# Splitting the transposing loads of two input matrices into rows 0-511 and 512-639

## The chip, the cores and the metric

One core of a Trainium2 chip. The time is the device time of the kernel in microseconds (us), as the median of several executions. The profile and the trace are of one execution: its span, from the first to the last instruction, is some 1.3 us shorter than the time that is measured for the same execution. PE is the matrix engine (TensorE), PEld its weight loads, DVE VectorE, ACT ScalarE, POOL GpSimd, SP the engine that issues most transfers.

## The reference, cut to what matters

The kernel computes a gated mix of a state space model (a) and a dense layer with GELU (b), for 2048 tokens of width 640:

```python
g = sigmoid((x * gate_w).sum(-1, keepdims=True))
Bu   = einsum("bld,pd->blp", x, B_bar)     # complex: B_re, B_im, both 640 x 640
h[t] = Lam_bar * h[t-1] + Bu[t]            # a scan along the tokens
a = 2.0 * einsum("blp,dp->bld", h, C).real + x * Dskip
b = gelu(x @ w1 + b1) @ w2 + b2
out = g * a + (1 - g) * b
```

The change concerns how B_re and B_im come into the core. As stored, a row is an output p and a column an input d; PE needs d on the partitions, so both are transposed while they are loaded.

## The kernel before

The kernel plans all its operations, sorts them by priority per engine and then emits them. Tokens of data (such as `("BT", 0)`) tie an operation to the load that it needs. The four parts that the argument touches, shortened:

```python
def load_T(name, sem, pairs, writes, prio, dur, lat=3.0, reads=()):
    def fn():
        for dst, src in pairs:
            t = dma_inc("sp", nc.sync.dma_start_transpose(dst, src), sem)
        return t
    return op(name, "sp", dur, reads, writes, fn, prio=prio, lat=lat)

def f_warm():                                   # keeps PE busy from 0.8 us on
    for n in (512,) * 6 + (256,):
        t = nc.tensor.matmul(PS[4][:, 0:n], one..., one..., start=True, stop=True)

for ci, src in enumerate((A_B_re, A_B_im)):     # the loads that are changed
    load_T(f"B{ci}", f"l_B{ci}", [(BT[:, ci, :, :], src)], [("BT", ci)], prio=30 + ci, dur=4.1)
xtrans(1, range(KD), 32, 3.4)                   # next block of x, transposed too
... (cut: gate weights, xnb, w2, C and so on, all on the same queue)

def bproj(q):                                   # 10 groups of 5 matmuls
    for ci in range(2):
        for k in range(KP):                     # KP = 5 blocks of 128 rows of B
            ... (cut: five matmuls over kd with BT[:, ci, kd, k*128:(k+1)*128] and xT[q])
            op(f"b_{q}_{k}{ci}", "pe", KD * d_mm(512), XT[q] + [("BT", ci)], [("bank", bank)], f_mm, ...)
```

PE's order at the start is: warm-up, eight 128-column transposes (L427), the first dense layer "m1" on the first block of tokens (L639 and L661, with the small L446 between), then the ten groups of `bproj(0)` (L704).

Of the kernel before, what the change touches and what calls it, by code (L numbers as in the profile page):

```python
# [147 lines left out]
class Prog:  # L148
# [8 lines left out]
    def op(self, name, eng, dur, reads, writes, fn, prio=None, lat=0.0, after=()):  # L157
        deps = {}
        for k in reads:
            for w in self.last_w.get(k, ()):  # L160
                deps[w.idx] = w
        for k in writes:
            for w in self.last_w.get(k, ()):
                deps[w.idx] = w
            for r in self.last_r.get(k, ()):
                deps[r.idx] = r
        for a in after:
            deps[a.idx] = a
        deps = list(deps.values())
        E = self.E  # L170

        def run(eg, deps=deps, eng=eng, fn=fn):
            E.wait(eng, *[d.done for d in deps if not (eng == "pe" and d.eng == "pe")])
            return fn()

        it = self.sch.add(name, eng, dur, deps, run, prio=prio, lat=lat)
        for k in writes:
            self.last_w[k] = [it]
            self.last_r[k] = []
        for k in reads:  # L180
            self.last_r.setdefault(k, []).append(it)
        return it


def bass_gated_mix__ssm_conv_s5__dense_activation_gelu__prompt_kernel(
# [18 lines left out]
    _, S, D = A_x.shape  # L204
# [3 lines left out]
    KD = D // 128  # L208
    KP = P // 128
# [16 lines left out]
    with ExitStack() as es:  # L226

        def SB(name, shape, dt):
            return es.enter_context(nc.sbuf_tensor(name, list(shape), dt))
# [5 lines left out]
        BT = SB("BT", [128, 2, KD, P], BF16)  # L235
# [72 lines left out]
        op = pr.op  # L308

        def inc(eng, ins):  # L310
            return E.inc(eng, ins, eng + "_s")

        def dma_inc(eng, ins, sem):
            SEM(sem)
            E.count.setdefault(sem, 0)
            ins.then_inc(sems[sem], 16)
            E.count[sem] += 16
            return (sem, E.count[sem])

        def d_act(n):  # L320
            return 0.26 + n * 0.00084
# [4 lines left out]
        def d_mm(n):  # L326
            return n / 2400.0 + 0.004
# [8 lines left out]
        def load_T(name, sem, pairs, writes, prio, dur, lat=3.0, reads=()):  # L336
            def fn():
                t = None
# [4 lines that stand above are left out]
# [10 lines left out]
        def xtrans(q, ks, prio, dur):  # L353
            load_T(f"xT{q}_{ks[0]}", f"l_xT{q}_{ks[0]}", [(xT[q][:, ks[0]:ks[-1] + 1, :], x2[q * 512:(q + 1) * 512, ks[0] * 128:(ks[-1] + 1) * 128])],
                   [("xT", q, k) for k in ks], prio, dur)
# [33 lines left out]
        for i, (nm, (r0, src)) in enumerate(ROWS.items()):  # L389
            src = src.rearrange("(k p) -> k p", p=128)  # L390
# [29 lines left out]
        for i, (k, c0, c1) in enumerate(((0, 0, 2), (0, 2, 4), (1, 0, 2), (1, 2, 4))):  # L420
            bank = (7, 6, 5, 4)[i]
# [18 lines left out]
        XT = {q: [("xT", q, k) for k in range(KD)] for q in range(1, NQ)}  # L440
# [137 lines left out]


        for ci, src in enumerate((A_B_re, A_B_im)):  # L580
            load_T(f"B{ci}", f"l_B{ci}", [(BT[:, ci, :, :], src)], [("BT", ci)], prio=30 + ci, dur=4.1)
        xtrans(1, range(KD), 32, 3.4)
        load("gwb", "sp", "l_gwb", gwb[:, :], gate_w.partition_broadcast(128), ["gwb"], prio=32.2)
        load("xnb", "sp", "l_xnb", xn[0][:, :, KN * 128:D], x2[0:512, KN * 128:D].rearrange("(c p) d -> p c d", p=128),
# [16 lines left out]
        def pe_prio():  # L601
            ctr["pe"] += 1
            return ctr["pe"]


        def next_bank():
            ctr["bank"] += 1
            return (ctr["bank"] - 1) % 8
# [87 lines left out]
        def bproj(q):  # L696
            for ci in range(2):
                for k in range(KP):
                    bank = next_bank()

                    def f_mm(k=k, ci=ci, bank=bank):
                        t = None
                        for kd in range(KD):
                            t = nc.tensor.matmul(PS[bank][:, :], BT[:, ci, kd, k * 128:(k + 1) * 128], xT[q][:, kd, :],  # L704
                                                 start=(kd == 0), stop=(kd == KD - 1))
                        return inc("pe", t)

                    op(f"b_{q}_{k}{ci}", "pe", KD * d_mm(512), XT[q] + [("BT", ci)], [("bank", bank)], f_mm, prio=pe_prio())

                    def f_ev(k=k, ci=ci, bank=bank):  # L710
                        dst = U[q % 2][:, :, ci, k, :]
                        src = PS[bank][:, :].rearrange("p (s t) -> p s t", s=2)
                        return inc("act", nc.scalar.activation(dst, src, ACT.Copy, scale=1.0 if ci == 0 else -1.0))  # L713

                    op(f"u_{q}_{k}{ci}", "act", d_act(512), [("bank", bank)], [("U", q % 2, k, ci)], f_ev, prio=10)
# [292 lines left out]
        m1_first()  # L1008
        m1(0, NW)
        bproj(0)  # L1010
        ssm(0)
        gates(0)
        m1(1)
        for q in range(0, NQ, 2):
            m1_tail(q)
        ssm(1)
        bproj(1)
        ssm(2)
        gates(1)
        outsT(0)  # L1020
        for q in range(2, NQ):
            ssm(2 * q - 1)
            bproj(q)
            ssm(2 * q)
            m1(q)
            xnload(q, "pool")
            gates(q)
            if q < NQ - 1:
                outsT(q - 1)
# [63 lines left out]
```

## Time and profile before

| | before |
|---|---|
| median of the first three runs | 213.13 us (212.79 to 213.13) |
| span of the profiled execution | 212.16 us |
| PE busy | 208.3 us, 98% |
| DVE busy | 190.1 us, 90% |
| real matrix: issued, landed | 9.91, 19.74 us |
| imaginary matrix: issued, landed | 16.21, 22.81 us |
| first matmul that needs them (L704) | 19.79 us |

"Landed" is when the transfer's completion semaphore has made all its 16 steps. The reading is the prediction's: a chain of work that is PE alone after 19.74, and one wait of PE for BT ahead of it. What the prediction does not show, and what will matter, is PE's timeline ahead of that wait (start, length, instructions, and in brackets the idle time before them with what ended it):

```profile
0.78 2.93 PE L415 MATMUL ps<-const-bfloat16-1.0 128*128 128x512 bf16 x7 [0.78 <-PEq L1078]
3.64 0.75 PE L427 MATMUL ps<-ident,xn 128*128 128x128 bf16 x8
5.25 2.54 PE L639 MATMUL ps<-xT,W1sb 128*128 128x256 bf16 x13 [0.86 <-DMA W1sb<-in_B_w_dram]
7.62 0.22 PE L446 MATMUL ps<-ident,rows 128*128 128x128 bf16 x1
7.68 6.42 PE L639 MATMUL ps<-xT,W1sb 128*128 128x512 bf16 x29
13.94 5.56 PE L661 MATMUL ps<-xT,W1sb 128*128 128x512 bf16 x25
```

From 5.25 us, when the first weights have come, m1 runs without a pause to 19.50. When m1 ends is therefore fixed by when it starts and by the clock in its first microseconds. Keep the 2.54 us of the first 13 matmuls of m1 in mind.

### The profile page before, as it was taken

Reading aid. Unit: us, or ns where it says so; the run is one execution under the profiler, and the core shown is the slowest. Engines: PE = TensorE matmul, PEld = TensorE weight load, DVE = VectorE, ACT = ScalarE, POOL = GpSimd, SP = SyncE. Lnnn points to the kernel's source line nnn. Section 1 sums busy time; section 2 is a strip of 40 time slices with the busy share of each in tenths; the row PEclk is TensorE's granted clock in tenths of the full one; section 3 lists DMA queues with packets and bytes.
Section 4 is the critical chain, followed back from the end, with each engine's and each line's share of the span. In section 5 each row is a group of like instructions: output and inputs, shape, how many; then the busy total and the mean of one; then the engine's idle time right before and its main releaser. Section 6 shows DMA issues by size and latency. Waiting matters only on the chain.

```text
span 212.2 us, 2747 instructions
## 1 busy us (share of the span) xinstructions
PE 208.3 (98%) x1102; PEld 104.4 (49%) x1102; DVE 190.1 (90%) x240; ACT 103.3 (49%) x177; POOL 4.2 (2%) x12
## 2 busy tenths in 40 slices
PE   6999999999999999999999999999999999999996
PEld 2444444444464444444464444444446444567775
DVE  2499999999999998999999999899999999499744
ACT  2388556679860253556681063455660027623330
POOL 1000000030000000000000000000010000000000
DMA  6899999998500020074263000009541000005251
GB/s 166 207 233 206 192 208 241 345 182 200 133 0 3 0 49 0 0 99 95 56 61 112 3 0 0 0 2 163 83 109 69 0 3 0 0 0 102 68 142 63
DMA packets 48744, 19.08 MB, mean 90 GB/s; under 512 B 41436, under 2 KB 47708, under 8 KB 48732
## 3 DMA queue, kind: packets, MB, share of 16 engines
q1 hardware_dynamic: 47072, 17.59, 39.3%
q0 software_dynamic: 1600, 1.32, 4.3%
q8 instruction: 8, 0.13, 0.3%
q14 instruction: 4, 0.03, 0.1%
q10 hardware_dynamic: 60, 0.01, 0.1%
HBM read 8.41 MB, written 2.63 MB: 52 GB/s over the span
## 4 chain that ended last, share of the span: by engine, by line
PE 90%; DMA 5%; SPq 4%; issue 0%; DVE 0%
PE ps L704 20%; PE ps L928 20%; PE ps L661 20%; PE ps L977 15%; PE ps L791 7%; PE ps L840 5%; DMA BT<-in_A_B_re_dram 5%; SPq L333 2%; SPq L340 2%; PE ps L682 1%; PE ps L939 1%; PE ps L805 0%; DVE W1sb L874 0%
## 5 line engine op out<-in xcount | busy, mean ns | idle before, releaser
L661 PE MATMUL ps<-xT,W1sb 128*128 128x512 bf16 x220 | 48.1, 379 | 0.0
L744 DVE TENSOR_TENSOR_SCAN W<-atab,V 128x1280 bf16<-128x1280 f32 x16 | 44.3, 2811 | 0.3
L704 PE MATMUL ps<-xT,BT 128*128 128x512 bf16 x200 | 43.8, 379 | 0.3 <-DMA BT<-in_A_B_re_dram 0.3
L928 PE MATMUL ps<-Gl,W2sb 128*128 128x512 bf16 (+1 forms) x234 | 42.7, 344 | 0.0
L668 ACT ACTIVATE Gl<-ps,cols 128x512 bf16<-128x512 f32 x44 | 29.9, 694 | 15.5 <-PE ps L661 15.5
L661 PEld LDWEIGHTS ps<-xT,W1sb 128*128 128x128 bf16 x220 | 21.5, 98 | 26.0
L977 PE MATMUL ps<-Hb,CT 128*128 128x512 bf16 x150 | 32.9, 379 | 0.0
L928 PEld LDWEIGHTS ps<-Gl,W2sb 128*128 128x128 bf16 x234 | 22.9, 98 | 19.3
L713 ACT ACTIVATE U<-ps 128x512 bf16<-128x512 f32 x40 | 23.7, 596 | 16.1 <-PE ps L704 16.0
L704 PEld LDWEIGHTS ps<-xT,BT 128*128 128x128 bf16 x200 | 19.4, 98 | 24.3 <-DMA BT<-in_A_B_re_dram 0.8
L946 ACT ACTIVATE E1T<-ps,cols 128x512 bf16<-128x512 f32 (+1 forms) x18 | 9.5, 624 | 36.0 <-PE ps L939 36.0
L977 PEld LDWEIGHTS ps<-Hb,CT 128*128 128x128 bf16 x150 | 14.4, 98 | 18.0 <-DVE V L496 0.6
L985 ACT ACTIVATE E2T<-ps 128x512 bf16<-128x512 f32 x15 | 9.1, 604 | 13.6 <-PE ps L977 13.6
L791 PE MATMUL ps<-W2sb,Gl 128*128 128x320 bf16 x104 | 14.8, 299 | 0.0
L614 DVE SCALAR_TENSOR_TENSOR trf<-xn,gwb 128x640 bf16<-128x640 bf16 x16 | 13.2, 823 | 0.4
L496 DVE TENSOR_TENSOR V<-V,W 128x1280 bf16<-128x1280 bf16 x16 | 12.5, 822 | 0.3
L496 DVE TENSOR_TENSOR Hb<-Hb,V 128x1280 bf16<-128x1280 bf16 x16 | 12.5, 822 | 0.3
L496 DVE TENSOR_TENSOR V<-mr,U 128x2560 bf16<-128x2560 bf16 x8 | 11.9, 1492 | 0.3
L791 PEld LDWEIGHTS ps<-W2sb,Gl 128*128 128x128 bf16 x104 | 10.1, 98 | 4.3 <-issue 0.3
L496 DVE TENSOR_TENSOR Hb<-c,W 128x2560 bf16<-128x2560 bf16 x8 | 11.9, 1491 | 0.2
L496 DVE TENSOR_TENSOR W<-mi,U 128x2560 bf16<-128x2560 bf16 x8 | 11.9, 1484 | 0.0
L496 DVE TENSOR_TENSOR V<-s,W 128x2560 bf16<-128x2560 bf16 x8 | 11.9, 1484 | 0.0
(91 smaller groups left out, 149.7 us busy)
## 6 DMA issues: line engine op xcount, KB each, us to landing
W2sb<-in_B_w_dram SPq DMA_DIRECT2D x1, 2080.0 KB, 8.6
out_dram<-xn SPq DMA_DIRECT2D x3, 640.0 KB, 4.8
xn<-in_A_x_dram POOLq DMA_DIRECT2D x2, 640.0 KB, 6.9
W1sb<-in_B_w_dram SPq DMA_DIRECT2D x3, 256.0 KB, 3.2
trf<-grow SPq DMA_DIRECT2D x3, 256.0 KB, 4.9
xn<-in_A_x_dram SPq DMA_DIRECT2D x1, 640.0 KB, 6.9
W1sb<-in_B_w_dram SPq DMA_DIRECT2D x1, 480.0 KB, 3.9
out_dram<-W1sb SPq DMA_DIRECT2D x3, 160.0 KB, 1.8
```

What stands on the lines that cost most here:

```text
L496: return inc("dve", nc.vector.tensor_tensor(out=o, in0=a, in1=b, op=o_))
L614: t = inc("dve", nc.vector.scalar_tensor_tensor(out=scr[:, :], in0=xn[q % 2][:, c, :], scalar=1.0, in1=gwb[:, :], op0=ALU.mult, op1=ALU.mu ...
L661: t = nc.tensor.matmul(PS[bank][:, :], W1sb[:, k, jf * 128:(jf + 1) * 128], xT[q][:, k, :], start=(k == 0), stop=(k == KD - 1))
L668: return inc("act", nc.scalar.activation(Gl[q % 2][:, jf, :], PS[bank][:, :], ACT.Gelu_apprx_tanh, bias=b1col[:, jf:jf + 1]))
L704: t = nc.tensor.matmul(PS[bank][:, :], BT[:, ci, kd, k * 128:(k + 1) * 128], xT[q][:, kd, :], start=(kd == 0), stop=(kd == KD - 1))
L713: return inc("act", nc.scalar.activation(dst, src, ACT.Copy, scale=1.0 if ci == 0 else -1.0))
L744: t = inc("dve", nc.vector.tensor_tensor_scan(out=g[:, ci, :], data0=a, data1=v[:, ci, :], initial=0.0, op0=ALU.mult, op1=ALU.add))
L791: t = nc.tensor.matmul(PS[bank][:, 0:HALF], Gl[q % 2][:, jf, t4 * 128:(t4 + 1) * 128], W2sb[:, jf, cols], start=False, stop=False, skip_gr ...
L840: t = nc.tensor.matmul(PS[bank][:, 0:n], H[b % NHB][:, ci, k, s * 128:(s + 1) * 128], CT[:, ci, k, cols], start=(i == 0), stop=(i == 2 * K ...
L928: t = nc.tensor.matmul(PS[bank][:, 0:t1 - t0], W2sb[:, jf, d * 128:(d + 1) * 128], Gl[q % 2][:, jf, t0:t1], start=(jf == 0), stop=False)
L946: return inc("act", nc.scalar.activation(E1T[:, d, t0:t1], PS[bank][:, 0:t1 - t0], ACT.Identity, bias=cols2[:, 0, d:d + 1]))
L977: t = nc.tensor.matmul(PS[bank][:, :].rearrange("p (s t) -> p s t", s=2), CT[:, ci, k, d * 128:(d + 1) * 128], Hb[:, 2 * (q % 2):2 * (q % ...
```

## The change

Its intent: `bproj` works block of rows by block of rows, but waited for all 640 rows of a matrix. With the rows in two transfers, the first four groups can start when the first 512 rows are there.

```diff
         for ci, src in enumerate((A_B_re, A_B_im)):
-            load_T(f"B{ci}", f"l_B{ci}", [(BT[:, ci, :, :], src)], [("BT", ci)], prio=30 + ci, dur=4.1)
+            for i, (p0, p1) in enumerate(((0, 512), (512, KP * 128))):
+                load_T(f"B{ci}{i}", f"l_B{ci}{i}", [(BT[:, ci, :, p0:p1], src[p0:p1, :])], [("BT", ci, i)],
+                       prio=30 + ci + 0.1 * i, dur=0.8 * (p1 - p0) / 128)
...
-                    op(f"b_{q}_{k}{ci}", "pe", KD * d_mm(512), XT[q] + [("BT", ci)], ...)
+                    op(f"b_{q}_{k}{ci}", "pe", KD * d_mm(512), XT[q] + [("BT", ci, k // 4)], ...)
```

The order of PE, DVE, ACT and POOL is the same in both builds. In the changed kernel every line number after the loads is one higher (L704 is L705).

More of the change, by code (lines that the diff above doesn't have):

```diff
@@ L580, in bass_gated_mix__ssm_conv_s5__dense_activation_gelu__prompt_kernel @@
         for ci, src in enumerate((A_B_re, A_B_im)):
-            load_T(f"B{ci}", f"l_B{ci}", [(BT[:, ci, :, :], src)], [("BT", ci)], prio=30 + ci, dur=4.1)
+            for i, (p0, p1) in enumerate(((0, 512), (512, KP * 128))):
+                load_T(f"B{ci}{i}", f"l_B{ci}{i}", [(BT[:, ci, :, p0:p1], src[p0:p1, :])], [("BT", ci, i)], prio=30 + ci + 0.1 * i, dur=0.8 * (p1 - p0) / 128)
         xtrans(1, range(KD), 32, 3.4)
@@ L706, in f_mm @@
                         return inc("pe", t)
-                    op(f"b_{q}_{k}{ci}", "pe", KD * d_mm(512), XT[q] + [("BT", ci)], [("bank", bank)], f_mm, prio=pe_prio())
+                    op(f"b_{q}_{k}{ci}", "pe", KD * d_mm(512), XT[q] + [("BT", ci, k // 4)], [("bank", bank)], f_mm, prio=pe_prio())
                     def f_ev(k=k, ci=ci, bank=bank):
```

## The prediction

> **What bounds the kernel now.** I read the page first: span 212.2 us, PE busy 208.3 us (98%), DVE 190.1 us (90%), DMA dense only in the first quarter. So either PE sets the end, or a chain that keeps PE fed does. The chain of work that ended last says which. Its columns are start, length and what held the chain; these are its pieces around the changed transposes and at its end:
>
> ```profile
> 9.34 0.53 SPq L333
> 9.86 0.04 issue
> 9.91 9.83 DMA BT<-in_A_B_re_dram
> 19.74 0.05 issue
> 19.79 10.97 PE ps L704 x50
> 30.75 14.03 PE ps L661 x65
> ...
> 204.73 5.47 PE ps L840 x50
> 210.21 0.03 issue
> 210.23 0.35 DVE W1sb L874
> ```
>
> Before 19.74 the chain runs through the SP queue and one transfer, the transpose of the real input matrix, issued at 9.91 and landed at 19.74. After it the chain is PE alone to 210.2, then one DVE step and a store. The chain gives this transpose 4.6% of the span, but that is not what it costs: until shortly before 19.74 PE was busy with other work. The cost is only PE's idle time there, so I asked for the waits of PE and for its timeline around that moment.
>
> ```profile
> PE ps L639 <- DMA W1sb<-in_B_w_dram: 0.9, 1, 0.9
> PE ps L415 <- PEq L1078: 0.8, 1, 0.8
> PE ps L704 <- DMA BT<-in_A_B_re_dram: 0.3, 1, 0.3
> ```
>
> These are all the waits of PE in the whole run: two at the start, before any changed instruction, and one of 0.3 us for BT. The imaginary matrix is not in the list.
>
> ```profile
> 18.26 1.24 PE L661 MATMUL ps<-xT,W1sb 128*128 128x512 bf16 x5
> 19.79 1.04 PE L704 MATMUL ps<-xT,BT 128*128 128x512 bf16 x4 [0.29 <-DMA BT<-in_A_B_re_dram]
> ```
>
> The 0.29 us counts from the modelled end of the previous matmul and is too small. Five matmuls took 1.24 us with 379 ns for one, so they start (1.24 - 0.379) / 4 = 0.215 us apart. The last one started at 19.50 - 0.379 = 19.12; the next could have started at 19.34 and started at 19.79. **The bubble is 0.45 us**, and I find no other after 5.3 us that isn't some 0.1 us at a change of row groups. This 0.45 us is all that the change can remove.
>
> **What the Trainium skill says.** "TensorE: Matmul & The Clock Gate", Part 1, gives 215.7 ns from start to start for 512 warm columns; the 215 ns above agree. "DMA: Bandwidth & Descriptors", Anatomy of one DMA, puts a fixed cost of about 2 us on a transfer, most of it between the last byte and the semaphore. The packet records of this trace agree in part: the data packets of the real matrix end by about 17.6, its semaphore is complete at 19.74 (2.1 us); for the imaginary one it is about 22.0 and 22.81 (0.8 us). "Advanced Engine Details and Errata", X-Bar Transpose (TRN2), expects 350 to 400 GB/s from a transposing transfer; here the pure transpose stretches show 268 to 275 GB/s, so I use these. The same section says that only one stream may transpose at a time; all four pieces stay on the SP queue, so this holds after the change.
>
> **The change, part by part.** The instruction order of the two builds differs only on SP: two transposes of 640 rows become four, of 512, 128, 512 and 128 rows. PE, DVE and ACT have the same lists. What changes is what PE waits for: groups k = 0 to 3 need the 512-row piece, k = 4 the 128-row piece.
>
> *What the first piece gains.* The matrix is 640 x 640 x 2 bytes = 819 kB, or 3,200 packets of 256 B; the first piece has 80% of it. The engines in windows around the transposes (columns: window, busy time of PE, PEld, DVE, ACT, POOL, granted clock, DMA share, GB/s):
>
> ```profile
> 15.00:17.50 2.50, 2.50 (x13) 1.18 (x12) 2.43 (x9) 2.50 (x6) 0.00 (x0) 1.00 1.19 268
> 17.50:19.50 2.00, 2.00 (x10) 0.69 (x7) 1.97 (x3) 2.00 (x4) 0.00 (x0) 1.00 0.90 86
> 19.50:22.00 2.50, 2.21 (x11) 1.04 (x12) 2.47 (x2) 1.36 (x3) 0.00 (x0) 1.00 1.21 274
> 22.00:23.50 1.50, 1.50 (x9) 0.68 (x8) 1.50 (x2) 0.86 (x2) 0.00 (x0) 1.00 0.96 162
> ```
>
> At 268 GB/s the 164 kB that the first piece lacks are 0.61 us, so it should land at 19.74 - 0.61 = 19.13. PE starts 0.05 us after the landing, so it is ready at 19.18, and wants the piece at 19.34. **The whole bubble goes, with 0.16 us to spare.** There may be more to spare: 17.5 to 19.5 is a hole (86 GB/s), in which the last packets of one transpose and the first of the next sit, and a 16 KB instruction fetch of 1.03 us begins at 17.83 on one DMA engine. Twelve of the 16 semaphore steps of the real matrix come only at 19.6 to 19.7, when the hole ends. If the hole is due to that fetch, the first piece, done by about 17.0, is past before it opens.
>
> *What it costs.* The trace has 512-row transposes of one 128-column block (1.12 to 1.20 us of issue) and of five (3.02 us where the queue didn't hold it up): 16 more 128x128 blocks for about 1.9 us, 0.12 us each, and some 0.65 us fixed. Two more transposes are about 1.3 us more of SP queue time. In the DMA stream every border between two transposes leaves a hole: at 17.5 to 19.5 it is 2 - 2 x 86 / 274 = 1.4 us, at 22.0 to 23.5 it is 1.5 - 1.5 x 162 / 274 = 0.6 us. So each added border is 0.6 to 1.4 us (estimate).
>
> *Whether the later pieces are in time.* A group of five matmuls is 5 x 0.216 = 1.08 us. From a start at 19.34, PE wants the second real piece at 19.34 + 4 x 1.08 = 23.7, the first imaginary one at 24.7, the second at 29.1, the next input block xT at 30.1. Estimated landings: second real piece 19.13 + 0.61 + 0.6 to 1.4 = 20.3 to 21.1; first imaginary 22.81 - 0.61 + one border = 22.8 to 23.6; second imaginary 24.0 to 25.6; xT 25.64 + two borders = 26.8 to 28.4. All are early, by at least 1.1 us.
>
> *What lies behind.* The loads after them come up to 2.8 us later: W2sb landed at 42.0 and is wanted by PE at 57.96. The narrowest is the small load of cols2 from POOL, which waits for W2sb, landed at 48.5 and is used by ACT at 49.48: ACT may stall up to 2 us here with evictions behind it. PE has eight banks and fills one in 1.08 us, and ACT soon has spare time, so this shouldn't reach PE.
>
> *DVE* works without a wait from 10 to 83.4 us, so it doesn't move when PE does. It delivers the states that PE wants at 72.67 at 67.98, and the last ones at 198.5 against 204.7. PE can come 0.45 us earlier everywhere without catching it. **The sum is -0.45 us**, and it goes through to the end because the chain is PE up to its last matmul: 213.13 - 0.45 = 212.68.
>
> **Rivals.**
> 1. *The bubble stays or shrinks only in part.* For it: if the late landing comes from the border with whatever transpose is behind (most of the semaphore steps came with the end of the hole), the new border sits behind the first piece just the same, and a 1.4 us hole there can give back the 0.61 us. Against it: the border after the imaginary matrix held its landing only 0.8 us, and the hole with the fetch in it comes at 17.8, after the first piece's data. It would make 212.9 to 213.2.
> 2. *A new wait takes its place*, for the first imaginary piece (margin 1.1 us) or xT (margin 1.7 us): two added borders of over 1.5 us each would do it. For it: the first hole was 1.4 us. Against it: the second was 0.6, and only one border counts for the imaginary piece. It would make 213 to 214.
> 3. *DVE becomes the bound*, at 90% busy. Against it: more than 4 us of slack at each point where PE takes its states. It would take away part of 0.45 us at most.
> 4. *The issue of the later loads is what counts* (cols2, ACT, banks). It would have to hold ACT for some 5 us; up to 1 us of loss if so.
>
> **Range and chances.** I give 75% to the whole gain, 12% to a part or none of it, 10% to a small new wait, 3% to something larger. The three times before spread over 0.34 us, as much as the gain, so the median may fall either side by 0.3. That makes 212.7, range 212.2 to 213.4. Faster by over 2% would need 4.3 us, and PE has only 0.45 us to give here besides its start: 1%. Slower by over 2% would need PE to stall 4.3 us: 1%.
>
> **What would show it.** In the changed profile: the wait of PE for BT gone from its list, L704 starting at about 19.3 with no idle time; the first piece landing between 17.5 and 19.2; the second before 23.7, imaginary ones before 24.7 and 29.1, xT before 30.1; the DVE timeline up to 83 us unmoved; PE's end some 0.45 us earlier; the number of busy PE microseconds unchanged. It is wrong if L704 still starts at 19.7 with a wait for the first piece (rival 1), if a wait appears at 23.7, 24.7 or 30 (rival 2), or if ACT or DVE stand as releasers of PE later on.

## The result, and the profile after

The changed kernel took 212.92 us (median of six, 212.51 to 213.45), beside 213.13 us of the kernel before (six, 212.79 to 213.54). The ratio is 0.9989, with a 95% interval of 0.9970 to 1.0007: the same within 2%, and a gain that this comparison can't tell from none. (A ratio is the mean time of one kernel's fast runs over that of the other's of the same rounds, so not quite the ratio of the medians.)

| | before | after |
|---|---|---|
| span of the profiled execution | 212.16 us | 212.13 us |
| first 512 real rows landed | 19.74 (all 640) | 17.29 |
| last 128 real rows landed | 19.74 | 18.65 |
| imaginary rows landed, first and last piece | 22.81 (all) | 22.86, 24.23 |
| next block of xT landed | 25.64 | 26.92 |
| PE's idle start time lost before the BT groups | 0.45 us | none |
| first BT matmul | 19.79 | 19.74 |

Here is the puzzle. The wait is gone, and yet the span is 0.03 us shorter, not 0.45. First the waits of PE after, all but the last that the view lists:

```profile
PE ps L415 <- PEq L1079: 0.8, 1, 0.8
PE ps L640 <- DMA W1sb<-in_B_w_dram: 0.5, 1, 0.5
...
```

No line for BT is left. (The view ends with 0.2 us on L705 put down to "issue": that is a record missing from the trace. The page counts 1,088 matmuls where the program has 1,102, and such a hole is exactly one matmul of 216 ns.) Then the chain that ended last, in order of time:

```profile
1.26 3.85 DMA W1sb<-in_B_w_dram
5.12 0.14 issue
5.25 2.94 PE ps L640 x13
...
14.51 5.40 PE ps L662 x25
19.90 3.45 PE ps L705 x16
...
204.67 5.47 PE ps L841 x50
210.17 0.35 DVE W1sb L875
```

Before, the chain went through SP's queue and the BT transpose up to 19.74. Now it is PE from 5.25 us to the end: the chain has left the transfers. And in PE's timeline of the changed kernel:

```profile
5.25 2.94 PE L640 MATMUL ps<-xT,W1sb 128*128 128x256 bf16 x13 [0.52 <-DMA W1sb<-in_B_w_dram]
...
14.34 5.56 PE L662 MATMUL ps<-xT,W1sb 128*128 128x512 bf16 x25
19.74 1.03 PE L705 MATMUL ps<-xT,BT 128*128 128x512 bf16 x4
```

The same 13 matmuls, started at the same 5.25 us, took 2.94 us instead of 2.54. In the trace, the five matmuls that start from 5.42 to 6.30 come up to 0.1 us later each than a matmul of their size needs at full rate (0.213 us instead of 0.109 for 256 columns); after that all is at full rate. So in this execution the clock of TensorE was at half rate until about 6.2 us, in the profiled execution of before only until 4.0. That made m1 end 0.40 us later, and 0.40 of the 0.45 us were gone before the BT groups began. Counting matmuls in two windows shows it (window, PE busy and matmuls, granted clock, DMA share, GB/s), before and after:

```profile
5.30:6.40 1.10, 1.10 (x8) 1.00 0.94 193
```

```profile
5.30:6.40 1.10, 1.10 (x6) 1.00 1.03 173
```

Eight matmuls against six, in windows that are equally "busy". The granted clock of the view reads 1.00 in both, so at the start of an execution it is the spacing of the matmuls that tells, not this column.

The transfers, in windows of the changed kernel (columns as in the prediction's table):

```profile
15.00:17.50 2.50, 2.50 (x13) 1.17 (x12) 2.40 (x11) 2.50 (x5) 0.00 (x0) 1.00 1.00 218
17.50:19.50 2.00, 2.00 (x11) 0.88 (x9) 2.00 (x2) 2.00 (x5) 0.00 (x0) 1.00 1.55 122
19.50:22.00 2.50, 2.50 (x13) 1.18 (x12) 2.43 (x3) 1.76 (x4) 0.00 (x0) 1.00 0.75 167
22.00:23.50 1.50, 1.45 (x8) 0.68 (x7) 1.50 (x2) 0.92 (x2) 0.00 (x0) 1.00 0.63 137
```

The hole that stood at 17.5 to 19.5 has moved: in the packet records, summed by 0.25 us, the rate is now under 15 GB/s from 19.25 to 20.5, inside the imaginary matrix, and the first real piece was in before it opened. So were the last 128 real rows, at 18.65. In this execution PE was ready for them only at 19.74, so that as far as the trace can tell even the unsplit matrix would have caused no wait here.

### The profile page after: what moved, and what is told of

Its sections match the earlier page's. It is cut to its first block, busy times and chain, and to the rows that moved or that the text cites. A ratio compares the mean times of both kernels' runs of the same rounds, so it can differ in the third digit from the quotient of the medians.

```text
span 212.1 us, 2737 instructions
## 1 busy us (share of the span) xinstructions
PE 208.0 (98%) x1088; PEld 104.9 (49%) x1102; DVE 190.1 (90%) x240; ACT 103.0 (49%) x177; POOL 4.2 (2%) x12
## 4 chain that ended last, share of the span: by engine, by line
PE 96%; DMA 2%; issue 1%; SPq 0%; DVE 0%
PE ps L662 22%; PE ps L705 20%; PE ps L929 20%; PE ps L978 15%; PE ps L792 7%; PE ps L841 5%; PE ps L640 4%; DMA W1sb<-in_B_w_dram 2%; PE ps L683 1%; PE ps L940 1%; PE ps L806 0%; SPq L333 0%; DVE W1sb L875 0%; PE ps L446 0%
## 5 line engine op out<-in xcount | busy, mean ns | idle before, releaser
L662 PE MATMUL ps<-xT,W1sb 128*128 128x512 bf16 x215 | 47.5, 379 | 0.3
L705 PE MATMUL ps<-xT,BT 128*128 128x512 bf16 x196 | 43.1, 379 | 0.3 <-issue 0.2
L929 PEld LDWEIGHTS ps<-Gl,W2sb 128*128 128x128 bf16 x234 | 22.9, 98 | 19.3
L705 PEld LDWEIGHTS ps<-xT,BT 128*128 128x128 bf16 x200 | 19.5, 98 | 23.7 <-ACT Gt L691 0.4
L714 ACT ACTIVATE U<-ps 128x512 bf16<-128x512 f32 x40 | 23.6, 599 | 14.6 <-PE ps L705 14.5
```

Of the source, the lines that this page charges most:

```text
L662: t = nc.tensor.matmul(PS[bank][:, :], W1sb[:, k, jf * 128:(jf + 1) * 128], xT[q][:, k, :], start=(k == 0), stop=(k == KD - 1))
L705: t = nc.tensor.matmul(PS[bank][:, :], BT[:, ci, kd, k * 128:(k + 1) * 128], xT[q][:, kd, :], start=(kd == 0), stop=(kd == KD - 1))
L714: return inc("act", nc.scalar.activation(dst, src, ACT.Copy, scale=1.0 if ci == 0 else -1.0))
L929: t = nc.tensor.matmul(PS[bank][:, 0:t1 - t0], W2sb[:, jf, d * 128:(d + 1) * 128], Gl[q % 2][:, jf, t0:t1], start=(jf == 0), stop=False)
```

## The experiments

The theory after the result (A): L704 starts at the later of two moments, the landing of the rows it needs plus 0.05 us, or the end of m1, which wanders with the first weights and the early clock. The time then is this start plus a constant. The split moves the first moment ahead of the second, so it gains what was waited, 0 to 0.45 us, depending on the execution. The rival (B): there is no gain, and the 0.03 us is all. A second question came with it: why the whole matrix landed as late as 19.74, by PE's instruction fetch (C) or by the border with the transpose behind it (D). (The trace shows 16 KB packets of the kind "instruction" on queue 8; that they are PE's instructions is inferred.) Twelve runs were made; none gave a wrong result.

All profiles in one table, from the instruction, semaphore and packet records of the traces. "Ready" is when the first BT matmul could have started, 0.216 us after the start of the last matmul of m1; "cold" what the half-rate clock cost m1; "fetch" the start of the first 16 KB instruction fetch after time zero.

| profile | first m1 | cold | ready | landed (first piece or whole) | BT start | lost | fetch | BT start to end |
|---|---|---|---|---|---|---|---|---|
| before | 5.25 | 0.00 | 19.34 | 19.74 | 19.79 | 0.45 | 17.83 | 192.38 |
| before2 | 5.19 | 0.00 | 19.68 | 18.38 | 19.68 | 0 | 19.70 | 192.37 |
| before3 | 4.64 | 0.24 | 18.97 | 19.26 | 19.30 | 0.34 | 17.23 | 192.38 |
| im_only | 4.62 | 0.00 | 18.71 | 19.11 | 19.16 | 0.46 | 17.06 | 192.37 |
| before_nops | 5.42 | 0.00 | 19.51 | 18.32 | 19.51 | 0 | 19.41 | 192.36 |
| before_nowarm | 4.50 | 2.07 | 20.65 | 18.36 | 20.65 | 0 | 20.61 | 192.37 |
| after | 5.25 | 0.39 | 19.74 | 17.29 | 19.74 | 0 | 18.84 | 192.40 |
| after2 | 4.65 | 0.30 | 19.03 | 17.25 | 19.03 | 0 | 17.43 | 192.40 |
| after3 | 4.69 | 0.07 | 18.86 | 16.85 | 18.86 | 0 | 17.09 | 192.41 |
| re_only | 4.63 | 0.68 | 19.41 | 17.55 | 19.41 | 0 | 18.51 | 192.36 |

The last column is the first finding: 192.36 to 192.41 us in ten profiles of six builds. Nothing after the start of the BT groups differs, so whatever the split does to the time is in that start.

### The same kernel again, and one half of the change alone

before2 is the kernel before, unedited; after2 the changed one. re_only splits the real matrix only, im_only the imaginary one only:

```diff
-for i, (p0, p1) in enumerate(((0, 512), (512, KP * 128))):
+for i, (p0, p1) in enumerate(((0, 512), (512, KP * 128)) if ci == 0 else ((0, KP * 128),)):   # re_only; ci == 1: im_only
-... XT[q] + [("BT", ci, k // 4)]
+... XT[q] + [("BT", ci, k // 4 if ci == 0 else 0)]
```

> The kernel before, once more, as a control. Theory A (the early clock): before the split, PE starts the BT groups at the later of two times, the landing of the real matrix plus 0.05 us (19.79) and the end of m1, which moves by 0 to about 1 us with the moment at which the TensorE clock leaves half rate. So the start of L704 stays near 19.8 if m1 is not later than that, and the wait for BT is 0.45 us less whatever m1 is late. Ratio to before 1.000, with an interval of some +-0.2%, which is as large as the effect of the split. Theory B (the split gains nothing and the 0.05 us between the two profiles is all there is): the wait stays 0.3 us by the profile in every execution.

> The changed kernel, once more. Theory A: no wait of PE for BT, the first real piece lands near 17.3, L705 starts as soon as m1 ends: at about 19.3 if the clock was at full rate by 5.3 us, at 19.7 or later if not. Ratio to before about 0.9985 to 0.9995: a gain between 0 and 0.45 us, about 0.2 on average. Theory B: ratio 1.000, and L705 starts at 19.7 or later for another reason than the early matmuls.

> Only the real matrix is split, the imaginary one is whole. Theory A: all of the effect is here. First piece lands near 17.3, no wait for BT, ratio as that of the changed kernel (0.9985 to 0.9995). Rival (the split of the imaginary matrix does part of the work, or its late landing costs): PE waits for the imaginary matrix near 24.6, or the ratio is above 1.000.

> Only the imaginary matrix is split. Theory A: as the kernel before: the real matrix lands at 19.7 +-0.3, the wait for it stays (0.45 us minus what m1 is late), the two pieces of the imaginary one land by 22.8 and 24.3, well before 24.7 and 29.1; ratio 1.000 within 0.2%. If the late landing of the real matrix is due to the border with whatever transpose is behind it and its size, a smaller piece behind it would make no difference either; if it is due to the instruction fetch near 17.8, the semaphore steps of the real matrix come after the hole as before.

Measured, all beside the same 11 runs of before (median 213.00 us): before2 213.16 us, ratio 1.0013 (0.9993 to 1.0032). after2 213.02 us, 1.0000 (0.9982 to 1.0018), where I had expected 0.9985 to 0.9995. re_only 213.33 us, 1.0030 (0.9998 to 1.0063), with one run of 215.48 us among six. im_only 212.82 us, 0.9992 (0.9971 to 1.0014). As feared, the intervals are as wide as the effect, so the times decide nothing here, and the profiles have to, one of each variant. im_only keeps the wait, as expected of a kernel whose real matrix is whole:

```profile
PE ps L705 <- DMA BT<-in_A_B_re_dram: 0.3, 1, 0.3
```

after2 and re_only have no such line. **So the effect, as far as there is one, comes from the split of the real matrix alone**; the imaginary pieces of im_only landed at 21.53 and 22.32, far ahead of their use. The ratio of re_only above 1 is outside what I expected; its profile gives a reason for that execution (0.68 us cold, the most of these four) but not for its six times, and I leave it open.

before2 was the surprise: the whole matrix landed at 18.38, not 19.74, and PE didn't wait at all, because m1 was late by a wait for its weights:

```profile
5.19 2.54 PE L639 MATMUL ps<-xT,W1sb 128*128 128x256 bf16 x13 [0.86 <-DMA W1sb<-in_B_w_dram]
...
12.56 1.89 PE L639 MATMUL ps<-xT,W1sb 128*128 128x512 bf16 x8 [0.46 <-DMA W1sb<-in_B_w_dram]
14.29 5.56 PE L661 MATMUL ps<-xT,W1sb 128*128 128x512 bf16 x25
19.68 1.03 PE L704 MATMUL ps<-xT,BT 128*128 128x512 bf16 x4
```

Its windows show where the hole went, with the fetch at 19.70 instead of 17.83:

```profile
15.00:17.50 2.50, 2.50 (x13) 1.11 (x12) 2.43 (x8) 2.50 (x5) 0.00 (x0) 1.00 1.16 263
17.50:19.50 2.00, 2.00 (x11) 0.91 (x10) 1.97 (x3) 2.00 (x5) 0.00 (x0) 1.00 2.34 191
19.50:22.00 2.50, 2.50 (x13) 1.15 (x12) 2.47 (x2) 1.70 (x3) 0.00 (x0) 1.00 0.35 76
```

191 GB/s at 17.5 to 19.5, where the kernel before had 86, and the hole (76 GB/s) behind the real matrix. The border between the two transposes is in nearly the same place (the real data end at about 17.2 instead of 17.6); the fetch has moved by 1.9 us. This speaks for C and against D.

### Without the warm-up, and an attempt to move the fetch

before_nowarm takes six of the seven warm-up matmuls away. before_nops adds empty instructions to PE's stream:

```diff
-for n in (512,) * 6 + (256,):          # before_nowarm
+for n in (256,):

+for _ in range(24):                    # before_nops, behind the warm-up, and one more at each matmul of m1_first
+    nc.tensor.nop(nofuse=True)
```

> The kernel before with some 70 empty instructions on PE's sequencer, 24 behind the warm-up and one at each early matmul, so that PE's next 16 KB of instructions are fetched earlier (near 12 us by my count instead of 17 to 19). Theory C (the late landing of the whole real matrix comes from that fetch, which holds one DMA engine for about 1 us while the next transpose begins): with the fetch gone from 17 to 19 us the real matrix lands at 17.7 to 18.6, unsplit, and PE doesn't wait for it. Theory D (it comes from the border with the transpose behind it): it still lands at 19.1 to 19.8 and PE waits 0.45 us less whatever m1 is late. The empty instructions themselves may delay PE by a few tenths in m1; time 212.4 to 213.6.

> The kernel before with one warm-up matmul instead of seven, so that the TensorE clock is surely at half rate when the real work starts. Theory A: m1 ends 1.5 to 3.5 us later (21 to 23), the wait for BT is gone without any split, time 214.2 to 216.2. Theory B: the wait for BT stays 0.3 us by the profile.

before_nowarm: the clock came to full rate at 8.7 us, m1 lost 2.07 us, the BT groups were ready only at 20.65 and found the whole matrix landed at 18.36. No wait for BT, without any split. That is theory A, made by hand: when m1 is late, there is nothing for the split to gain. (m1 was 1.3 us later than in before, and the time was 214.01 us; I had expected 1.5 to 3.5 us and 214.2 to 216.2.) The ratio to before was 1.0004 (0.9933 to 1.0076), an interval that says little: two of the seven runs of before on that chip took 215.41 us, for a reason that no profile shows. The profile's span, 213.02 us, agrees with 20.65 + 192.37.

before_nops failed as an experiment. The trace records none of the added instructions, so I can't say that they ran, and the fetch came at 19.41, not near 12. As an observation it counts: late fetch, landing at 18.32, no wait (213.29 us, ratio 0.9977, 0.9908 to 1.0046).

Put together, the six whole real matrices in the table: with the fetch at 17.06, 17.23 and 17.83 they landed at 19.11, 19.26 and 19.74, each 1.9 to 2.1 us after the start of the fetch; with the fetch at 19.41, 19.70 and 20.61 they landed at 18.32, 18.38 and 18.36, whatever the fetch. The second real piece of the split kernels does the same: fetch at 17.09 and 17.43, landed at 19.24 and 19.58; fetch at 18.51 and 18.84, landed at 18.23 and 18.65. The first pieces (16.85 to 17.55) were early in all four. **In these four the split got the first four blocks of rows in ahead of the fetch.** The fetch as the cause is an inference from executions in which it moved by itself; I found no clean way to move it alone. The packet records show what goes with it: around this fetch 11 to 22 packets of 256 B of the transposes took over 0.8 us each, in each of the 14 traces, where some 18 ns are usual. In before they end at 19.6 us, which is when twelve of the 16 semaphore steps of the real matrix come. In 13 traces the first such packet starts 0.04 to 0.85 us after the fetch; but in before2 it starts at 19.20, ahead of the fetch at 19.70, and such packets also occur near 28 us, with no fetch on that queue there. So a stop of the transposes is shown, and that it comes with the fetch; that the fetch causes it is not. Why it moves between 17.1 and 19.7 in kernels with the same PE order is open too.

### A wait that is always there, to measure the gain of the split

If PE always waits, the landing alone sets the start. In the "late" twins the load of xnb (384 KB) goes ahead of the matrices, in the "later" twins the transpose of xT's second block:

```diff
-load("xnb", ..., 32.4, dur=1.0, lat=6.0, reads=["xna"])     # before_late, after_late
+load("xnb", ..., 29.5, dur=1.0, lat=6.0, reads=["xna"])

-xtrans(1, range(KD), 32, 3.4)                               # before_later, after_later
+xtrans(1, range(KD), 29, 3.4)
```

> The kernel before with the load of xnb (384 KB, wanted only at 49 us) put ahead of the two transposes, so that PE waits for the real matrix in every execution, whatever the early clock does. Theory A: the real matrix lands 1 to 2 us later (20.5 to 21.7), PE waits for it 1.0 to 2.3 us beyond the end of m1, the span grows by just that less 0.45: about 213.7 to 214.8 us. From the start of L704 to the end of the span 192.4 us as in every profile so far. Theory B (PE's start of L704 isn't what sets the end): the span stays near 212 although L704 starts later.

> The changed kernel with the same load ahead. Theory A: now the whole gain of the split shows, as PE waits in both: the first piece lands 0.6 us (640 packets less) to 1.4 us (if the unsplit one is also held by the instruction fetch) earlier than the whole matrix of the same order, L705 starts that much earlier, ratio to its unsplit twin 0.993 to 0.997; no later wait, as the imaginary piece is wanted 5.4 us after the first. Theory B: the twins differ by less than 0.2 us.

> The kernel before with the transpose of the second block of xT (wanted at 30 us) ahead of the two input matrices. The real matrix should then land at 21 to 22.5 us, behind the fetch of PE's instructions at 17 to 20 and far behind the latest end of m1 seen (19.8 to 20.0), so that every execution waits for it and neither the early clock nor the fetch hides the effect of the split. Theory A: PE waits some 1.5 to 3 us, the span is the start of L704 plus 192.4, about 214 to 215 us, timed 215 to 216. If PE's clock falls back in the wait, somewhat more.

> The changed kernel with the same transpose ahead. Theory A (the first piece is ready sooner by the 640 packets it lacks, about 0.6 us, and PE turns that into time): first piece 0.5 to 0.8 us before the whole matrix of its twin, L705 as much earlier, no further wait at the later pieces, timed 0.4 to 0.9 us less than its twin (ratios to before that differ by 0.002 to 0.004). Rival (the border behind the first piece holds its landing as it holds the whole one's, or the later pieces come too late): the same time as its twin, or a new wait for the second real or the first imaginary piece.

The late twins: whole matrix landed at 20.54, first piece at 19.57, BT groups from 20.59 and 19.61, spans 212.97 and 212.02 us. The 0.97 us of the landing are 0.94 us of the span. But they are not the split's alone. The fetch began at 18.27 in one and at 17.50 in the other, both times as the data of the first transfer ended, and the landings came 2.3 and 2.1 us after it. In after_late the fetch thus held the first piece as it holds a whole matrix: the split doesn't always get ahead of it. But after_late waited only 0.17 us, so the margin was again too thin for all executions, and the times show it: 214.18 and 214.07 us, ratios to before 1.0038 (0.9937 to 1.0140) and 0.9998 (0.9929 to 1.0068). The 0.993 to 0.997 between the twins that I expected is in the two profiled executions (213.34 and 214.28 us), not in the medians.

The later twins: whole matrix at 22.99 (I had expected 21 to 22.5), first piece at 21.95, 1.04 us apart. Here too the fetch differs: at 18.52, in the middle of the whole matrix, and at 19.96, at the end of the first piece, which landed 2.0 us later. How much of the 1.04 us is the split's is therefore open. Waits of PE for BT, unsplit and split:

```profile
PE ps L704 <- DMA BT<-in_A_B_re_dram: 4.1, 1, 4.1
```

```profile
PE ps L705 <- DMA BT<-in_A_B_re_dram: 2.1, 1, 2.1
```

Times 217.49 (215.90 to 219.52; I had expected 215 to 216) and 216.84 us (215.52 to 217.58), ratios to before 1.0174 (1.0141 to 1.0206) and 1.0153 (1.0122 to 1.0184). The ratios differ by 1.0174 - 1.0153 = 0.2% or 0.45 us, at the low end of what I expected, and the two intervals overlap: the times alone don't show a gain. There is more in these spans than the landing: 217.10 and 214.41 us differ by 2.7. The unsplit execution shows this after its wait (windows, columns as before):

```profile
19.50:23.00 3.50, 0.00 (x0) 0.00 (x0) 3.43 (x4) 0.20 (x1) 0.00 (x0) 1.00 0.88 162
23.00:24.50 1.50, 1.47 (x7) 0.72 (x8) 1.47 (x2) 0.17 (x1) 0.00 (x0) 0.96 1.28 288
24.50:28.00 3.50, 3.50 (x11) 1.23 (x9) 3.46 (x3) 1.02 (x2) 0.00 (x0) 0.53 0.98 148
```

After 4.1 us without a matmul the granted clock was at half from 24.37 to 27.78 us (0.53 is the mean of the last window), and seven matmuls came some 427 ns apart, two more in part: 1.7 us lost on top (2.7 = 1.04 + 1.7). With the 2.1 us wait of the split execution it stayed at 1.00 (four of its five other executions have a mean clock of 0.992, so they lost it too; how long they waited is not recorded). By mean clock of the whole span, and without one unsplit execution (219.52 us, 0.984), executions of the same kind compare thus: at 0.992, 217.68 us unsplit (mean of four) and 217.09 split (four); at 1.000, 215.90 (one) and 215.64 (two). That is 0.6 and 0.3 us. All agree in sign, and none is sharp enough to call the gain shown.

### Both kernels once more, and all times pooled

> The kernel before for a third profile, on one chip with the changed one. What the runs so far say: the real matrix, whole, lands at 18.3 to 18.4 where PE's instruction fetch comes after 19 us, and at 19.1 to 19.7 where it comes between 17 and 18, and PE waits only if m1 ends before that. So here: landing 19.1 to 19.8 if the fetch starts before 18.2, 18.2 to 18.5 if after 19; a wait only in the first case; the end of the span 192.4 us after the start of L704; ratio 1.000 +-0.002.

> The changed kernel for a third profile. First piece lands at 17.2 to 17.6 whatever the fetch does, no wait for BT, L705 starts 0.22 us after the last matmul of m1, the end of the span 192.4 us later. Over all timed executions of both kernels (pooled) the mean gain is 0.1 to 0.3 us, since only the executions with an early fetch and a full clock have a wait to lose; in this job alone the interval will hold 1.000.

before3 213.01 us, ratio 0.9992 (0.9977 to 1.0007); after3 212.65 us, 0.9989 (0.9966 to 1.0012). The profile of before3 came as expected, with the fetch at 17.23, landing at 19.26 and 0.34 us lost. That of after3 has no wait, as expected, and a BT start at 18.86 that no unsplit profile reached; its first piece landed at 16.85, ahead of the 17.2 to 17.6 that I gave. Pooled over the three jobs in which both ran: 40 executions of before with a mean of 213.07 us, 18 of after with 212.90. **The gain is 0.17 us, with +-0.20 as a 95% interval from the spread of both**: in line with A, not proof against B by times alone. The profiles say more: among four whole-matrix profiles with PE's stream unedited (before, before2, before3, im_only) the loss was 0.45, 0, 0.34 and 0.46 us, mean 0.31; among four with the real matrix split, 0. These are different executions, though, with different fetches and early clocks. Within the split ones an estimate is possible: the last real rows landed before PE was ready in after and re_only (18.65 against 19.74, 18.23 against 19.41), and after it in after2 and after3 (19.58 against 19.03, 19.23 against 18.86). If a whole matrix had landed with its last rows, the split saved 0, 0, 0.60 and 0.42 us, 0.26 on average (estimate).

## Why the prediction was right or wrong

**What bounds the kernel: right.** PE's idle start time before L704 is all that the change could remove; from L704 on, the ten profiles of the table are the same within 0.05 us. (Of the twins only before_later differs, with 194.06 us, by its fall of the clock.)

**The bubble goes: right, by a wider margin and partly for another reason.** The first piece was to land at 19.13 by the size of the missing rows, or earlier if the hole belonged to the fetch. It landed at 17.29, just below the window of 17.5 to 19.2 that I gave. The second branch held: where the fetch was late, even the whole matrix landed at 18.3 to 18.4, so the rows themselves are about 1 us (18.4 against 17.3) and what goes with the fetch the remaining 1.4 us of the 2.45 between the two first profiles (an estimate from other executions). The 0.61 us for the missing rows came from windows that hold a part of a hole: inside the transposes the view `--dma` of 9.5 to 21 us has slices of 285 to 293 GB/s, not 268 to 275, which makes it 0.57 us. And that no wait stood in the first profile after was luck: PE was ready so late there that, as far as the trace can tell, the split had nothing to save.

**The sum, -0.45 us: the term that was mis-sized.** I wrote that "the sum is -0.45 us, and it goes through to the end". I took the 19.34 at which PE could have started, and the 19.74 of the landing, from one execution as if they were properties of the kernel. Both wander: ready from 18.71 to 19.74, landing of the whole matrix from 18.38 to 19.74 (profiles with PE's stream unedited). The loss averaged 0.31 us in four profiles and the times show 0.17 +-0.20. The statement that L704 would start "at about 19.3" failed with it: it started at 19.74 in the first profile, and at 19.03 and 18.86 in the next two. None of my four rivals had this in it: no new wait took the place of the old one, but PE's own late start did. The point forecast of 212.7 was 0.2 us too low, in the range of 212.2 to 213.4.

**Rival 1 (the border gives the gain back): it did not happen in the order as built.** The semaphore of the first piece was complete 0.7 us after its last data packets, with the second piece right behind it. In after_late, where the fetch fell on that border, it took 2.1 us from the last data on; so the rival's hold exists, but it takes the fetch as well as the border.

**Rival 2 (a new wait) and the later pieces: no wait came.** The second real piece landed at 18.65 (I had 20.3 to 21.1), the imaginary ones at 22.86 and 24.23 (22.8 to 23.6, 24.0 to 25.6), xT at 26.92 (26.8 to 28.4, wanted at 30.1). The borders were overcharged: xT came at 25.64, 26.56 and 25.30 in the three profiles of before and at 26.92, 26.35 and 26.03 in those of after, on average 0.6 us later for two more borders, 0.3 each where I had said 0.6 to 1.4. Each three spread over about 1 us, so the 0.3 is rough.

**Rival 4 (cols2 holds ACT): it happened, and cost nothing.** In the changed kernel the trace has

```profile
ACT xT L966 <- DMA cols<-in_A_Dskip_dram: 1.3, 1, 1.3
```

which isn't in the list of before. I had said up to 2 us, and that eight banks would keep it from PE; they did.

**Rival 3 and DVE: right in what matters, wrong in a detail.** DVE never stood as the releaser of an idle PE (of weight loads it did in both kernels, 0.3 us at a time for the states and 0.8 to 1.0 us once near the start). But its timeline didn't stay put: its first step on the BT results began at 34.43 instead of 34.03, because the small transpose of the parameters on PE (L446), which feeds DVE, came 0.4 us later as well.

## What to carry to other kernels

A wait of a few tenths is worth the gap between two moments that both vary from execution to execution. Before pricing it, take a second profile and look at what sets each of them; a gain of 0.45 us from one profile may be 0.2 us on average. When a wait disappears and the time stays, compare where the engine stood *before* the wait: the loss may have moved ahead of it. And to price a part that is hidden half of the time, build a twin in which it never hides, but keep the waits short enough that nothing else, here the clock, changes with them, and look in both twins at what else moved, here the fetch.

## What the Trainium skill lacked or had wrong

- "TensorE: Matmul & The Clock Gate", Part 1, says that full rate comes after a busy window of about 3.4 us that runs freely, so that its moment differs from run to run. The runs agree (full rate at 4.0 us before, 6.2 us after, with the same warm-up from 0.78 us), and a wait of 4.1 us brought half rate back in one execution, one of 2.1 us didn't in another. It does warn that the count of slow matmuls differs between runs of one kernel, and that the clock events of a trace can't be fully trusted. What it lacks is the size that is left behind a warm-up of 2.9 us: 0 to 1.0 us between executions here (1.0 in after_later), as much as many a change is worth. It also lacks that the granted clock of a profile can read 1.00 while matmuls are 427 ns apart at the start: in before the trace has no clock record at all, in im_only the first is at 4.56 us.
- "DMA: Bandwidth & Descriptors", Anatomy of one DMA, describes the fixed cost of a transfer that GpSimd issues, and puts most of it down to the receipt of the last byte; the transposes here are issued by SP. No page has it that a 16 KB instruction fetch on one of the 16 engines (0.9 to 1.3 us) at the border of two transposes goes with a semaphore that is complete 1.8 to 2.1 us after the last data instead of 0.7 to 1.2.
- "Advanced Engine Details and Errata", X-Bar Transpose (TRN2), expects 350 to 400 GB/s; the transposes here ran at 285 to 293 GB/s in the slices that hold nothing else, and at 268 to 275 in windows with a part of a border. The 261 GB/s that "DMA: Bandwidth & Descriptors", Latency and other measured facts, gives for a non-contiguous middle dimension is nearer. No page gives the cost of one more border between two transposes on one queue, about 0.3 us here (a rough mean of three profiles each).
